# A two-layer token mixer on one core: weight decode without TensorE, and chunk 1's inverse in 16x16 blocks

## Chip, core and metric

The kernel runs on one core of a Trainium2 chip. The metric is the device time of one execution in microseconds. An execution's span runs from its first to its last instruction in the profile. The engines are TensorE (PE; PEld its weight loads), VectorE (DVE), ScalarE (ACT), GpSimd (POOL) and SyncE (SP), which issues most of the DMAs.

## What is computed

Three stages follow one another for 4 x 768 = 3072 tokens with 8 heads of 48 values, 384 in all:

```python
for t in range(S):                                   # S = 768, per batch and head
    y[t] = q[t] @ state                              # k_n = k / (|k| + 1e-6)
    v_old = state.T @ k_n[t]
    state = state + beta[t] * outer(k_n[t], v[t] - v_old)
h = y @ w_in                                         # 384 x 2048
g = where(h >= 1, h, where(h <= -1, 0, (h + 1)**2 / 4))
x = g @ w_out                                        # 2048 x 384
xn = x / sqrt(mean(x*x) + 1e-6) * rms_g
out = (silu(xn @ w_gate) * (xn @ w_val)) @ w_out2    # 1536 wide
```

The weights are float64. The kernel gets them as 64-bit integers and rebuilds from each a float32 and its split into two parts for TensorE: hi, the value rounded to the matmul's format, and lo, the rest.

## The kernel before

**Chunks.** The 768 steps are done in 12 chunks of 64. Per chunk, each of two batch pairs (a unit u = 2 * chunk + pair) goes through the same steps: a_ss and a_coef (norms of k, factors), ka_load and a_gram (Gram matrix of k on TensorE, scaled by nn into al and written to memory as scr_a), an inverse of the unit triangular matrix, a_mz and a_mw (blocks of the inverse, two small TensorE steps), b_load, b_q, b_vn, b_gs (products with state and queries, masked by VectorE), b_tr (the inverse applied), b_x (the chunk's output), b_ds (the new state) and b_xT (transpose to the layer's layout: hi part xh by ScalarE, rest xl by VectorE). Chunk after chunk depends on the state.

**Inverses.** inverse(g) (L510) takes 32x32 blocks of two or four units: 31 steps of two operations on GpSimd over (31 - j)(j + 1) elements. inv0 (L455) is for chunk 0 alone: 16x16 blocks, 15 steps of two operations on VectorE, and the step from 16 to 64 rows is done in b_tr by small matmuls with off, y and z (L644 to L670). Chunk 1 is inverse(1), with a_mz and a_mw behind it.

**First layer.** m1(j, f) works on the tokens of chunk j and 128 of the 2048 columns: nine matmuls into hps (three each of hi*hi, hi*lo, lo*hi), ScalarE's two passes and VectorE's maximum w_ for the activation, a rounding g and its rest, then nine matmuls into acc. The 16 tiles f of a chunk run in order, and chunk j + 1 only behind chunk j. hps has two buffers, given back by w_.

**Weight decode.** w_dec(1, f, i) makes the first layer's 32 weight pieces (128 x 384), w_dec(2, f, i) the second layer's 36, which go back to memory (w2d) and are read again later. Per piece: ScalarE writes the scaled high word y and, into every second 16-bit value of a, its half-precision form with sign and exponent (L275, L276). VectorE shifts y left by 3 and ors in a (L286), masks out the exponent (L287) and multiplies the low word by it (L297, for the second layer L290 and L291 on a copy of the piece that a second load shifts by 16 bits, L271). For the first layer ScalarE then rounds y to hi (L300), TensorE forms y - hi + lo in PSUM by three matmuls with identities (L315 to L317, wlo) and ScalarE or VectorE copies that to lo (L320, L322).

**Order.** Nothing is scheduled at run time: the class Flow plays the stages in Python when the program is built, with a cost and an engine per stage, priorities, and counted buffers, and writes each engine's instructions in the order that comes out. An engine runs its instructions in that order, so one that waits holds up all that stand behind it. In idle time before the first layer TensorE gets dummy matmuls (warm, L866). A stage can name a second engine (alt), and Flow takes the one that is free first.

After the last chunk the second layer runs over six blocks of 512 tokens (m2_l1, m2_l2), with its weights read back from memory.

Of the kernel before, what the change touches and what calls it, by code (L numbers as in the profile page):

```python
# [23 lines left out]
C = 64  # L24
# [30 lines left out]
class Flow:  # L55
# [30 lines left out]
    def start(self, p):  # L86
        key, st, i = p[1], p[3], p[4]
        t = self.free.get(st.eng, 0.0)
# [11 lines left out]
        return t  # L100
# [60 lines left out]
def kernel_body(  # L161
# [14 lines left out]
    stg = ctx.enter_context(tc.tile_pool(name="stg", bufs=4))  # L176
# [54 lines left out]
    def consts2():  # L231
# [19 lines left out]
    def w_dec(n, f, i):  # L251
        if n == 2:
            needs = [("w_dec", 1, NF1 - 1, 1)]
        else:
            needs = [("a_gram", EARLY - 1)] if f + SK * i > 14 else []
        if n == 1:
            needs = needs + ([("inv0", 1 if f + SK * i < 9 else 19)] if f + SK * i >= 4 else [])
        me = ("w_dec", n, f, i)
        mem = "wp" if n == 1 and f + SK * i < 10 else "stg"
        yield S("SP", (1, 1.09) if n == 1 else (2, 2.18), needs, (mem,) * n)  # L260
# [814 lines left out]
```

## Time and profile before

| | us |
|---|---|
| median of 3 runs | 1155.97 (1154.07 to 1157.64) |
| span of the profiled execution | 1152.4 |
| PE busy in the span | 1107.5 (96%) |
| DVE / ACT / POOL busy | 661.8 / 569.9 / 286.3 |

The page gives the profiled execution's span and no total of its own; the runs lie 1.7 to 5.2 us above it. Busy is the time in which an engine executes something; in stretches of the span the shares differ a great deal, so the rows below are by stretch. A row of the timeline has start, length, engine, line, operation, output <- input, shapes and, in brackets, idle time before it with what ended it.

### The profile page before, as it was taken

What the parts mean: (1) busy time and instruction counts of PE and PEld (TensorE: products, weight loads), DVE (VectorE), ACT (ScalarE), POOL (GpSimd) and SP (SyncE); (2) the same over time, 40 slices, a digit from 0 to 9 for tenths busy, and PEclk for the clock granted to TensorE, in tenths of its full rate; (3) what the DMA queues carried; (4) which work ended last, traced back from release to release, by engine and by line L of the source; (5) the groups of instructions that cost most, each with busy time, mean ns of one, the idle gap of its engine ahead of it and who ended that gap; (6) DMA issues with size and microseconds to landing.
All of it is one profiled execution on the core that took longest, in us unless ns stands there. A gap on an engine that the chain in (4) does not pass through costs nothing.

```text
span 1152.4 us, 27191 instructions
## 1 busy us (share of the span) xinstructions
PE 1107.5 (96%) x11224; PEld 996.4 (86%) x11224; DVE 661.8 (57%) x1337; ACT 569.9 (49%) x1360; POOL 286.3 (25%) x479
## 2 busy tenths in 40 slices
PE   8979999999999999999999999999999999999998
PEld 7857888899998999899999999788888888888887
DVE  6797876786877876785775453443433333333333
ACT  4677877765765767567665464222212122122212
POOL 3282865858348114811000000000000000000000
PEclk9989999999999999999999999999999999999999
DMA  7945587784786556385440564001001010010000
GB/s 219 285 143 138 148 262 197 231 208 153 185 224 185 128 199 181 114 206 172 151 148 2 183 207 167 10 23 37 19 1 46 10 37 19 1 46 10 28 1 28
DMA packets 165099, 136.97 MB, mean 119 GB/s; under 512 B 115056, under 2 KB 126064, under 8 KB 164976
## 3 DMA queue, kind: packets, MB, share of 16 engines
q1 hardware_dynamic: 141536, 132.31, 38.2%
q10 hardware_dynamic: 23440, 2.93, 1.7%
q8 instruction: 88, 1.44, 0.5%
q14 instruction: 35, 0.29, 0.1%
HBM read 100.88 MB, written 34.34 MB: 117 GB/s over the span
## 4 chain that ended last, share of the span: by engine, by line
PE 74%; DVE 11%; ACT 4%; POOL 3%; DMA 3%; issue 2%; SPq 1%; DVEq 0%; POOLq 0%; ACTq 0%
PE acc L736 9%; PE gv L736 8%; PE gv L737 8%; PE gv L738 8%; PE acc L737 8%; PE acc L738 8%; PE hps L736 4%; PE hps L737 4%; PE hps L738 4%; PE gs L623 2%; POOL xi L536 2%; PE px L691 2%; POOL tmp L530 2%; PE tr L678 1%; DVE da L287 1%
## 5 line engine op out<-in xcount | busy, mean ns | idle before, releaser
L752 ACT ACTIVATE xh<-fix 128x512 fp32r<-128x512 f32 x72 | 45.5, 632 | 333.7 <-PE acc L738 328.4
L753 DVE TENSOR_TENSOR xl<-fix,xh 128x512 fp32r<-128x512 f32 x72 | 49.9, 694 | 270.6 <-ACT xh L752 270.6
L736 PE MATMUL hps<-xh,w 128*128 128x256 f32 x576 | 167.5, 291 | 9.9 <-DVE w__1065 L773 2.2
L737 PE MATMUL acc<-g,w 128*128 128x256 f32 x576 | 164.7, 286 | 10.6 <-DVE g L781 10.4
L736 PE MATMUL acc<-g,w 128*128 128x256 f32 x576 | 167.8, 291 | 2.7 <-ACT g L779 2.7
L736 PE MATMUL gv<-fix,w 128*128 128x512 f32 x432 | 168.2, 389 | 0.7 <-DVE fix L978 0.7
L737 PE MATMUL gv<-fix,w 128*128 128x512 f32 x432 | 168.1, 389 | 0.0
L738 PE MATMUL gv<-fix,w 128*128 128x512 f32 x432 | 168.1, 389 | 0.0
L737 PE MATMUL hps<-xl,w 128*128 128x256 f32 x576 | 164.2, 285 | 0.0
L738 PE MATMUL hps<-xh,w 128*128 128x256 f32 x576 | 163.9, 285 | 0.0
L738 PE MATMUL acc<-g,w 128*128 128x256 f32 x576 | 163.5, 284 | 0.0
L769 ACT ACTIVATE s<-hps 128x256 f32<-128x256 f32 x192 | 73.6, 384 | 108.3 <-PE hps L738 104.2
L736 PEld LDWEIGHTS hps<-xh,w 128*128 128x128 f32 x576 | 111.2, 193 | 13.7 <-DVE w__1065 L773 2.6
L737 PEld LDWEIGHTS acc<-g,w 128*128 128x128 f32 x576 | 110.7, 192 | 13.0 <-DVE g L781 12.9
L530 POOL TENSOR_TENSOR tmp<-nt,xi 128x87 f32<-128x87 f32 (+21 forms) x186 | 104.4, 561 | 54.5 <-DMA nt<-scr_a 40.4
L736 PEld LDWEIGHTS acc<-g,w 128*128 128x128 f32 x576 | 110.4, 192 | 6.1 <-ACT g L779 2.9
L536 POOL TENSOR_TENSOR xi<-xi,tmp 128x87 f32<-128x87 f32 (+21 forms) x186 | 110.4, 594 | 14.6
L737 PEld LDWEIGHTS hps<-xl,w 128*128 128x128 f32 x576 | 111.4, 193 | 0.3 <-DVE xl L732 0.3
L738 PEld LDWEIGHTS hps<-xh,w 128*128 128x128 f32 x576 | 111.3, 193 | 0.0
L738 PEld LDWEIGHTS acc<-g,w 128*128 128x128 f32 x576 | 110.7, 192 | 0.0
L770 ACT ACTIVATE s<-s,vhalf 128x256 f32<-128x256 f32 x192 | 97.9, 510 | 6.2
L736 PEld LDWEIGHTS gv<-fix,w 128*128 128x128 f32 x432 | 81.1, 188 | 17.8 <-DVE fix L978 1.1
(747 smaller groups left out, 2156.5 us busy)
## 6 DMA issues: line engine op xcount, KB each, us to landing
wst<-in_w SPq DMA_DIRECT2D x68, 384.0 KB, 4.6
w2d<-wst SPq DMA_DIRECT2D x36, 384.0 KB, 4.1
w<-w2d SPq DMA_DIRECT2D x36, 384.0 KB, 6.0
wsv<-in_w SPq DMA_DIRECT2D x36, 383.5 KB, 5.5
kvb<-in_kv SPq DMA_DIRECT2D x22, 384.0 KB, 5.5
kt<-in_kqT SPq DMA_DIRECT2D x24, 256.0 KB, 4.2
scr_a<-al SPq DMA_DIRECT2D x24, 256.0 KB, 3.9
qs<-in_kqT SPq DMA_DIRECT2D x48, 128.0 KB, 4.3
```

The costliest lines, as they stand in the source:

```text
L287: nc.vector.tensor_scalar(out=a, in0=yf, scalar1=0xFF800000, scalar2=None, op0=ALU.bitwise_and)
L530: nc.gpsimd.tensor_tensor(out=tv, in0=nt[:, m:32, j:m].to_broadcast([w, n, m]), in1=x[:, j:m, 0:m].to_broadcast([w, n, m]), op=ALU.mult,)
L536: nc.gpsimd.tensor_tensor(out=x[:, m:32, 0:m], in0=x[:, m:32, 0:m], in1=tv, op=ALU.add)
L623: nc.tensor.matmul(out=ps[half(b), h, 0:n], lhsT=kt[u][half(1 - b), 4 * k + h, :], rhs=qs[p][half(1 - b), b, 4 * k + h, 0:n], start=True, ...
L691: nc.tensor.matmul(out=ps[half(b), h, 0:D], lhsT=t[:, 0:C], rhs=v, start=True, stop=True)
L736: nc.tensor.matmul(out=out, lhsT=wh, rhs=xh, start=first, stop=False, skip_group_check=shared)
L737: nc.tensor.matmul(out=out, lhsT=wh, rhs=xl, start=False, stop=False, skip_group_check=shared)
L738: nc.tensor.matmul(out=out, lhsT=wl, rhs=xh, start=False, stop=last, skip_group_check=shared)
L752: nc.scalar.activation(out=hi, in_=src, func=ACTF.Copy)
L753: nc.vector.tensor_tensor(out=lo, in0=src, in1=hi.bitcast(F32), op=ALU.subtract)
L769: nc.scalar.activation(out=s, in_=ps, func=IDENTITY_SAT240, scale=240.0)
L770: nc.scalar.activation(out=s, in_=s, func=ACTF.Square, bias=vhalf, scale=1.0 / 480.0)
```

## The change

- Decode: ScalarE writes both halves of a: the upper as before, and into the lower 16 bits a third pass that scales the low word to three bits (L266 of the new text). One shift-or then gives the whole float32. hi is rounded by ScalarE or VectorE (alt), and VectorE subtracts: lo = y - hi. The mask, the multiplication, the three matmuls, the copy from PSUM, the second load and the zeroing of a are gone; both layers use the same code. The staging pool has 3 buffers, not 4.
- Chunk 1: inv0 becomes inv16(c) for c = 0 and 1. For chunk 1 its 15 steps run on GpSimd; b_tr takes the 16-row path for both chunks; inverse(1), a_mz and a_mw of chunk 1 are gone.
- a_gram's scaling al for later chunks may run on VectorE in one operation instead of ScalarE's eight.
- Flow: priorities of w_dec and a small change of how start times are counted. The order of all engines comes out anew.

```diff
@@ class Flow
-    CHAIN = {"b_tr": 4, "b_x": 4, "b_xT": 4, "inverse": 2, "a_mz": 4, "a_mw": 4}
+    CHAIN = {"b_tr": 4, "b_x": 4, "b_xT": 4, "inverse": 3, "inv16": 2, "a_mz": 4, "a_mw": 4}
...
-        t = self.free.get(st.eng, 0.0)
+        t = 0.0
...
-        return t
+        return max(t, self.free.get(st.eng, 0.0))
@@ w_dec
-        yield S("SP", (1, 1.09) if n == 1 else (2, 2.18), needs, (mem,) * n)
+        yield S("SP", (1, 1.09), needs, (mem,))
...
-            sv = stg.tile([128, 4 * DM], U16, name="wsv", tag="wst")
-            nc.sync.dma_start(out=sv[:, 0:4 * DM - 2], in_=w2[f, :, DM * i:DM * i + DM].bitcast(U16)[:, 1:4 * DM - 1])
...
-        nc.scalar.activation(out=y.bitcast(F32), in_=wf[:, :, 1], func=ACTF.Copy, scale=2.0**-112)
-        nc.scalar.activation(out=a.bitcast(F16).rearrange("p (n t) -> p n t", t=2)[:, :, 1], in_=wf[:, :, 1], func=ACTF.Copy, scale=2.0**-60)
+        ends = a.rearrange("p (n o) -> p n o", o=1).bitcast(U16)
+        nc.scalar.activation(out=y.bitcast(F32), in_=w_hi, func=ACTF.Copy, scale=2.0**-112)
+        nc.scalar.activation(out=ends[:, :, 1].bitcast(F16), in_=w_hi, func=ACTF.Copy, scale=2.0**-60)
+        nc.scalar.activation(out=ends[:, :, 0], in_=w_lo, func=ACTF.Copy, scale=0.874 * 2.0**-29, bias=0.5)
...
-        nc.vector.scalar_tensor_tensor(out=yf, in0=y, scalar=3, in1=a, op0=ALU.logical_shift_left, op1=ALU.bitwise_or)
-        nc.vector.tensor_scalar(out=a, in0=yf, scalar1=0xFF800000, scalar2=None, op0=ALU.bitwise_and)
...
-        nc.vector.scalar_tensor_tensor(out=lo, in0=w0, scalar=2.0**-52, in1=a.bitcast(F32), op0=ALU.mult, op1=ALU.mult)
+        nc.vector.scalar_tensor_tensor(out=y, in0=y, scalar=3, in1=a, op0=ALU.logical_shift_left, op1=ALU.bitwise_or)
         dac.append(a)
-        yield S("ACT", 0.41)
-        nc.scalar.activation(out=hi, in_=y.bitcast(F32), func=ACTF.Copy)
+        yield S("ACT", 0.41, alt=[("DVE", 0.35)])
+        if fl.eng == "ACT":
+            nc.scalar.activation(out=hi, in_=y.bitcast(F32), func=ACTF.Copy)
+        else:
+            nc.vector.tensor_copy(hi, y.bitcast(F32))
+        yield S("DVE", 0.5, (), (), ("dec",))
+        nc.vector.tensor_tensor(out=lo, in0=y.bitcast(F32), in1=hi.bitcast(F32), op=ALU.subtract)
...
-        nc.tensor.matmul(out=ps, lhsT=ident, rhs=y.bitcast(F32), start=True, stop=False)
-        nc.tensor.matmul(out=ps, lhsT=ineg_r, rhs=hi, start=False, stop=False)
-        nc.tensor.matmul(out=ps, lhsT=ident_r, rhs=lo, start=False, stop=True)
@@ a_gram
-            yield S("ACT", 1.65, [("a_coef", g)], ("wp" if ew else "al",), ("at",))
+            yield S("ACT", 1.65, [("a_coef", g)], ("wp" if ew else "al",), ("at",), alt=[("DVE", 0.6)])
@@ inv16 (was inv0)
+    def inv16(c):
+        us = (2 * c, 2 * c + 1)
+        name, eng = ("POOL", nc.gpsimd) if c else ("DVE", nc.vector)
...
-            eng = nc.scalar if k in (1, 3, 5) else nc.sync
-            eng.dma_start(out=nt[o:o + 16], in_=scr_a[0][o:o + 16, :, :, c:c + 16].rearrange("t u h s -> (u h) t s"))
+            q = nc.scalar if k in (1, 3, 5) else nc.sync
+            q.dma_start(out=nt[o:o + 16], in_=scr_a[c][o:o + 16, :, :, r:r + 16].rearrange("t u h s -> (u h) t s"))
...
-            yield S("DVE", 0.37 + n * m * 2 / 960)
+            yield S(name, 0.36 + n * m * 0.004 if c else 0.37 + n * m * 2 / 960)
@@ b_tr
-        if c == 0:
+        if c < 2:
...
+            for b in range(2):
+                nc.scalar.activation(out=qs[p][half(b), b, :, C:C + D], in_=ps[0][half(b), :, 0:D], func=ACTF.Copy)
@@ the list of work
-        fl.add(PG[0] + 6, inv0)
+        fl.add(PG[0] + 6, inv16, 0)
...
-                fl.add(p0 + 6, inverse, g)
+                fl.add(p0 + 6, *((inverse, g) if g > 1 else (inv16, 1)))
...
-            if a:
+            if a > 1:
                 att(p0, a, ((-8, a_mz), (-5, a_mw)))
...
-                fl.add(f + SK * i + (-14), w_dec, 1, f, i)
+                fl.add(f + SK * i - 5, w_dec, 1, f, i)
```

TensorE's order at the entry of the first layer, before; xps is the transpose of a unit, ds its new state, hps the first tile:

```order
L691 MATMUL px<-z,qs 64x48 x16
L705 MATMUL ds<-z,kvb 48x48 x16
L723 MATMUL xps<-ident,xs 128x128 x3
L705 MATMUL ds<-z,kvb 48x48 x16
L315 MATMUL wlo<-dy,ident 128x384
L316 MATMUL wlo<-w,ineg_r 128x384
L317 MATMUL wlo<-w,ident_r 128x384
```

and with the change, up to the first tile:

```order
L702 MATMUL xps<-ident,xs 128x128 x3
L636 MATMUL tr<-z,y 32x48 x16
L684 MATMUL ds<-z,kvb 48x48 x16
L670 MATMUL px<-z,qs 64x48 x16
L684 MATMUL ds<-z,kvb 48x48 x16
L702 MATMUL xps<-ident,xs 128x128 x3
L401 MATMUL gk<-ka 64x64 x48
L715 MATMUL hps<-xh,w 128x256
```

The weight groups between the transposes and the tiles (another one follows before the first hps, and more between the tiles) are gone, and Gram matrices stand there. Further on, the first a_mw of chunk 2 stood ahead of the ninth tile of the first layer's chunk 1 and stands ahead of the fifth.

VectorE's order around xl, the rest of a unit's transpose, before; L286, L287 and L297 are one piece's decode:

```order
L732 TENSOR_TENSOR xl<-xps,xh 128x3x128
L286 SCALAR_TENSOR_TENSOR dy<-dy,da_100 128x384
L287 TENSOR_SCALAR da_100<-dy 128x384
L297 SCALAR_TENSOR_TENSOR w<-wst,da_100 128x384
L712 TENSOR_TENSOR qs<-ds,qs 48x8x48 x2
L732 TENSOR_TENSOR xl<-xps,xh 128x3x128
L712 TENSOR_TENSOR qs<-ds,qs 48x8x48 x2
```

and with the change; nt_715 is the copy of chunk 1's inverse that GpSimd makes in x_625:

```order
L274 SCALAR_TENSOR_TENSOR dy<-dy,da_100 128x384
L280 CAST w<-dy 128x384
L282 TENSOR_TENSOR w<-dy,w 128x384
L457 COPY nt_715<-x_625 128x256
L711 TENSOR_TENSOR xl<-xps,xh 128x3x128
L691 TENSOR_TENSOR qs<-ds,qs 48x8x48 x2
L412 TENSOR_TENSOR al<-gk,nn 128x512 x3
```

Between the two units' xl the copy of chunk 1's inverse has come in, and the scalings al of later chunks stand behind.

ScalarE's order where chunk 0's inverse is applied (z), with the change; the DMA row is three of the loads of chunk 1's blocks:

```order
L264 ACTIVATE dy<-wst 128x384
L265 ACTIVATE da_98<-wst 128x384
L266 ACTIVATE da_98<-wst 128x384
L627 ACTIVATE z<-tr 128x384
L352 ACTIVATE kk<-kk 128x384 x4
L443 DMA nt_715<-scr_a_556 16x16x16 x3
L641 ACTIVATE z<-tr 128x384
```

Before, chunk 1's blocks were loaded by SyncE alone, and nothing but a rounding stood between these two z.

## Rows read from the trace of the kernel before

**Rows 1.** Stretches: length, busy us (instructions) of PE, PEld, DVE, ACT, POOL; PEclk, DMA share, GB/s

```profile
0.00:58.50 58.50, 50.73 (x842) 45.33 (x843) 42.17 (x114) 32.77 (x71) 19.42 (x50) 1.00 0.84 254
58.50:159.00 100.50, 87.01 (x1075) 74.76 (x1074) 78.85 (x151) 78.20 (x211) 69.59 (x110) 0.95 0.58 163
159.00:703.00 544.00, 524.76 (x7339) 508.28 (x7338) 379.86 (x827) 356.37 (x896) 197.30 (x321) 0.99 0.61 177
703.00:1152.40 449.40, 445.02 (x1976) 368.09 (x1974) 160.92 (x247) 102.52 (x183) 0.00 (x0) 1.00 0.06 21
```

**Rows 2.** TensorE's timeline: first tiles of chunks 0 and 1, two weight groups

```profile
58.53 0.28 PE L736 MATMUL hps<-xh,w 128*128 128x256 f32 x1
...
88.59 0.81 PE L315 MATMUL wlo<-dy,ident 128*128 128x384 f32 x2
...
89.59 0.81 PE L315 MATMUL wlo<-dy,ident 128*128 128x384 f32 x2
...
158.97 0.28 PE L736 MATMUL hps<-xh,w 128*128 128x256 f32 x1
```

**Rows 3.** Line L317 in 58.5 to 159: count, duration min/median/max, starts

```profile
L317 PE MATMUL wlo<-w,ident_r x24: 331/335/522, 58.4 to 140.3; 128*128 128x384 f32 x24
```

**Rows 4.** VectorE's waits in 58.5 to 159: us, times, longest

```profile
DVE g L781 <- ACT g L779: 5.9, 4, 3.2
DVE w L322 <- PE wlo L317: 5.8, 5, 4.3
```

**Rows 5.** SyncE's timeline: loads of chunk 1's blocks

```profile
43.27 2.64 SPq L521 DMA_DIRECT2D nt<-scr_a  x4
```

**Rows 6.** GpSimd's timeline: chunk 1's inverse starts; the next starts and ends

```profile
48.75 0.25 POOL L530 TENSOR_TENSOR tmp<-nt,xi 64x31 f32<-64x31 f32 x1 [27.37 <-DMA nt<-scr_a]
49.08 0.26 POOL L536 TENSOR_TENSOR xi<-xi,tmp 64x31 f32<-64x31 f32 x1
...
118.90 0.25 POOL L530 TENSOR_TENSOR tmp<-nt,xi 128x31 f32<-128x31 f32 x1 [2.71 <-DMA nt<-scr_a]
...
160.59 0.25 POOL L536 TENSOR_TENSOR xi<-xi,tmp 128x31 f32<-128x31 f32 x1
```

**Rows 7.** VectorE by line in 58.5 to 159: busy us, mean ns | idle before

```profile
L297 DVE SCALAR_TENSOR_TENSOR w<-wst,da 128x384 fp32r<-128x384 uint32 x20 | 14.9, 746 | 0.7
L286 DVE SCALAR_TENSOR_TENSOR dy<-dy,da 128x384 uint32<-128x384 uint32 x20 | 14.8, 739 | 0.4 <-ACT da L276 0.4
L287 DVE TENSOR_SCALAR da<-dy 128x384 uint32<-128x384 uint32 x20 | 11.0, 551 | 0.7
L322 DVE CAST w<-wlo 128x384 fp32r<-128x384 f32 x10 | 5.5, 551 | 5.9 <-PE wlo L317 5.8
...
L633 DVE TENSOR_TENSOR qs<-gs,mask 64x256 f32<-64x256 f32 x8 | 3.3, 419 | 0.1
...
L732 DVE TENSOR_TENSOR xl<-xps,xh 128x384 fp32r<-128x384 f32 x3 | 1.5, 541 | 0.0
```

**Rows 8.** ScalarE by line in 58.5 to 159

```profile
L276 ACT ACTIVATE da<-wst 128x384 f16<-128x384 f32 x22 | 13.9, 633 | 0.0
L445 ACT ACTIVATE al<-gk,nn 128x64 f32<-128x64 f32 x64 | 13.7, 367 | 2.6 <-DVE nn L404 2.6
L275 ACT ACTIVATE dy<-wst 128x384 f32<-128x384 f32 x22 | 12.1, 550 | 2.2 <-PE wlo L315 2.2
L300 ACT ACTIVATE w<-dy 128x384 fp32r<-128x384 f32 x20 | 10.3, 523 | 4.1 <-DVE dy L286 4.0
```

**Rows 9.** Line L447, the al that VectorE makes: min/median/max ns

```profile
L447 DVE TENSOR_TENSOR al<-gk,nn x4: 681/691/692, 10.4 to 37.6; 128x512 f32<-128x512 f32 x4
```

**Rows 10.** VectorE's timeline: a shift-or during GpSimd's inverse, and one without

```profile
77.55 0.97 DVE L286 SCALAR_TENSOR_TENSOR dy<-dy,da 128x384 uint32<-128x384 uint32 x1
...
95.14 0.55 DVE L286 SCALAR_TENSOR_TENSOR dy<-dy,da 128x384 uint32<-128x384 uint32 x1
```

**Rows 11.** TensorE's timeline: the first a_mw of chunk 2

```profile
183.98 1.20 PE L569 MATMUL mg<-tx,g 32*32 32x32 f32 x64
```

More of the change, by code (lines that the diff above doesn't have):

```diff
@@ L252, in w_dec @@
         if n == 2:
-            needs = [("w_dec", 1, NF1 - 1, 1)]
+            needs = [("m1", 0, NF1 - 1)]
         else:
@@ L256, in w_dec @@
         if n == 1:
[L257 to L260 removed]
+            needs = needs + ([("inv16", 0, 1 if f + SK * i < 9 else 19)] if f + SK * i >= 4 else [])
+        mem = "wp" if n == 1 and f + SK * i < 13 else "stg"
+        yield S("SP", (1, 1.09), needs, (mem,))
         if mem == "wp":
@@ L309, in w_dec @@
-        yield S("PE", 1.0, (), (bank,), ("dec",))
-        if pre:
-            fl.pre += 1
-            ps = accp.tile([128, 512], F32, name="wlo", tag=f"acc{fl.pre % 2}")[:, 0:DM]
-        else:
-            ps = ap_.tile([128, DM], F32, name="wlo", tag="at")
-        nc.tensor.matmul(out=ps, lhsT=ident, rhs=y.bitcast(F32), start=True, stop=False)
-        nc.tensor.matmul(out=ps, lhsT=ineg_r, rhs=hi, start=False, stop=False)
-        nc.tensor.matmul(out=ps, lhsT=ident_r, rhs=lo, start=False, stop=True)
@@ L318, in w_dec @@
-        yield S("ACT", 0.45, (), (), (bank,), alt=[("DVE", 0.58)])
-        if fl.eng == "ACT":
-            nc.scalar.activation(out=lo, in_=ps, func=ACTF.Copy)
-        else:
-            nc.vector.tensor_copy(lo, ps)
-        w1t[f, i] = t
+        yield S("SP", (1, 1.09), (), (), ("stg",), lag=3.0)
+        w2d[f, i] = dram.tile([128, 2, DM], F32, name=f"w2d{f}_{i}", tag=f"w2d{f}_{i}")
+        nc.sync.dma_start(out=w2d[f, i], in_=t.bitcast(F32))
     def w_in(f, i, pool_):
@@ L652, in b_tr @@
                     nc.tensor.matmul(out=py[half(b), h, :], lhsT=o[half(b), h, :], rhs=dt[half(b), h, :], start=True, stop=True)
-            if u == 0:
-                inv["y"] = p1.tile([128, 2, H, C], F32, name="y", tag="ka")
+            if p == 0:
+                inv["y"] = p1.tile([128, 2, H, C], F32, name="y", tag="y")
             yield S("ACT", 0.38, [("b_tr", u, 0)], ("wt",))
@@ L668, in b_tr @@
                         )
-                yield S("ACT", 0.38, (), (), ("at",) + (("ka",) if u else ()) if k == 2 else ())
-                nc.scalar.activation(out=z, in_=ps[0][:, :, 0:D], func=ACTF.Copy)
-            us0[u] = z
+                if k < 2:
+                    yield S("ACT", 0.38)
+                    nc.scalar.activation(out=z, in_=ps[0][:, :, 0:D], func=ACTF.Copy)
+            end = ("at",) + (("y",) if p else ())
+            if c == 0:
+                yield S("ACT", 0.38, (), (), end)
+                nc.scalar.activation(out=z, in_=ps[0][:, :, 0:D], func=ACTF.Copy)
+                us0[u] = z
+                return
+            yield S("ACT", 0.76, (), (), end + ("wt",))
+            for b in range(2):
+                nc.scalar.activation(out=qs[p][half(b), b, :, C:C + D], in_=ps[0][half(b), :, 0:D], func=ACTF.Copy)
             return
-        yield S("PE", 1.27, [k for v in (u, u ^ 1) for k in (("a_mw", v), ("b_gs", v, 0, i), ("b_gs", v, 1, i), ("b_vn", v))], ("at",), ("wt",))
+        yield S("PE", 1.27, [k for v in (u, u ^ 1) for k in (("a_mw", v), ("b_gs", v, 0, 1), ("b_gs", v, 1, 1), ("b_vn", v))], ("at",), ("wt",))
         ps = ap_.tile([128, H, C], F32, name="tr", tag="at")
@@ L787, in m1 @@
         else:
[L788 to L789 removed]
+            yield S("PE", 1.08, [("w_dec", 1, f, 1)], ("acc",), ("g", "wp") if j == NB - 1 else ("g",), dp=SK)
         m1_l2(j, f)
```

142 lines of the change are left out of this document (57 added, 85 removed).

## Prediction

> **What bounds the kernel now.** I read the stretches first, then the waits of the engines inside the worst stretch, then single rows. The stretches [rows 1] cut the 1152.4 us at three rows of TensorE [rows 2]: the first matmul of the first layer's chunk 0 (58.53), the first of its chunk 1 (158.97), and the second layer's first at 703, where the third stretch ends. The reader is to see that the stretches are bound by different things. The last one has TensorE busy for 445.02 of 449.40 us. In the third, 524.76 of 544.00 us are busy, so at most 19.2 us could be won there without less work. The second stretch is the odd one: 100.50 us for one chunk of the first layer, of which the third stretch does eleven in 544.00. TensorE is busy 87.01 us in it, but weight groups are part of that: 24 have their last matmul in it, one of them at the very border [rows 3], so I count 23, and one group is 1.00 us from its first matmul to that of the next [rows 2]. VectorE is busy 78.85 us, ScalarE 78.20, GpSimd 69.59: nothing is saturated, and the four engines wait for each other in turn. VectorE's waits [rows 4] name the partners: 5.8 us for the three matmuls of a weight group, 5.9 us for ScalarE's rounding of g. The change takes hold in this stretch, so the sum is made by stretches.
>
> **The change, part by part.**
>
> *The way to the first matmul (58.5 us).* Removed are nine weight groups on TensorE, but they stood in time that dummy matmuls fill anyway: nothing. VectorE's decode before the inverse of chunk 0 is shorter by the mask, which the chain behind feels as 2 to 3 us. Against it stand two new in-order waits that the order shows. On ScalarE the three loads of chunk 1's blocks stand ahead of chunk 0's z. They wait until the scaled Gram blocks have landed in memory; the loads that now do the same on SyncE are issued at 43.27 [rows 5] and feed GpSimd at 48.75 [rows 6]. On VectorE the copy of chunk 1's inverse stands ahead of the second xl, without which the first matmul's partner cannot run. GpSimd does that inverse now in 30 operations of at most 64 elements; its first two, of 31 elements, take 0.25 us and start 0.33 us apart [rows 6], and I allow 0.37 on the mean: some 11 us, so it ends near 59.5. Copy and xl (0.54 [rows 7]) bring the first layer to about 60: **+1.5 us**, bounds -2 (the copy never waits) and +4 (the loads land 3 us later).
>
> *Chunk 0 of the first layer (100.5 us).* TensorE loses 23 groups of 1.00 us and gains about 4 us of small matmuls (chunk 1's 16-row steps less its 32-row ones), so its own work falls from 87.0 to 68. ScalarE loses the eight-fold al (13.7), most of the roundings (15 of 20, at 0.523: 7.8) [rows 8] and its copies from wlo. The third pass costs at most the 0.633 us of the second, which has the same input and also writes 16-bit values two apart; between that and the first pass's 0.550 I take 0.633. For the 14 groups that the new order leaves behind the first tile, three passes are 14 x 1.816 = 25.4 us against 26.0 now. ScalarE falls below 57 us. It stops being a partner to wait for.
>
> VectorE is what remains. Busy time removed in the stretch: the three decode operations of 20 groups and ten copies from PSUM, 14.8 + 11.0 + 14.9 + 5.5 = 46.2; the four products behind a_mw, priced as a mask (0.419), 1.7 [rows 7]; second-layer decode that now comes later, one group and a half, about 3. Together 50.9. Added, by counting VectorE's new order from the second xl to the sixteenth w_: 18 groups with shift-or (0.739) and subtraction (two inputs in SBUF like L297, so 0.746), 15 roundings (as L287, 0.551): 35.0; eight al at 0.691 [rows 9]: 5.5; chunk 2's eight masks and four subtractions, which came later, at 0.419: 5.0; chunk 1's dt, y and m, priced as al: 2.9. Together 48.4. So 78.85 - 50.9 + 48.4 = 76. **VectorE's work in this stretch hardly changes; what changes is that it no longer stops for TensorE.** GpSimd corrects this a little. A shift-or takes 0.97 us while GpSimd runs an inverse and 0.55 while it does not [rows 10]; xl, which reads PSUM, has a mean of 0.541 [rows 7]. Chunk 1's inverse now runs before the stretch; the 32-row one for chunks 2 and 3 moves into it from 118.9 to 160.6 [rows 6]. I expect it from about 75 to 117, over 11 of the 18 groups, not nearly all of them: 74 us. Bounds: 64 (none meets GpSimd) and 79 (all do).
>
> Idle time of VectorE is now 100.5 - 78.85 = 21.65 us. The 5.8 us for weight groups goes, and most of the waits for ScalarE should too; I keep 4 us for the last tiles, where TensorE's 2.2 us a tile is the pace. Bounds 2 and 21.65. The stretch becomes 74 + 4 = 78: **-22.5 us**, bounds 66 and 100.
>
> The Trainium skill (SBUF — State Buffer, "Who interferes with whom") says that a VectorE operation with two SBUF inputs, or in a two-port mode, and a GpSimd operation that reads SBUF exclude each other for the whole instruction. This trace agrees on which operations suffer, but shows a mean loss of some 0.19 us in an operation, not a whole GpSimd instruction. The rule speaks against this change, since the new subtraction and rounding are of the exposed kinds and the PSUM copy that they replace was not. With the row's loss the stretch is 78 us; with a full block of 0.6 us for each of 33 operations it would be some 90.
>
> *Chunks 1 to 11 (544 us).* TensorE has the same tiles and the same attention steps here. ScalarE trades 96 al pieces for 35 third passes, VectorE takes 12 al and loses one of four decode operations, and one load of 384 KB in two goes. All of it lies beside TensorE. I take **-3 us** of the 19.2 us that it idles; bounds -10 and +7.
>
> *Second layer (449.4 us).* Untouched: 0.
>
> Sum: 60 + 78 + 541 + 449.4 = 1128.4 us of span, 24 us less. The page records no total beside its span; the median of the runs, 1155.97, lies 3.6 us above the span, which I take as start and end. So **1132 us**.
>
> **Rivals.**
>
> *TensorE sets the stretch after all.* If VectorE's idle time and most of the meeting with GpSimd vanish, the stretch falls to TensorE's 68 us and the later ones gain 6: 60 + 68 + 538 + 449.4 + 3.6 = **1119**. For it: ScalarE is relieved by a quarter and more, and chunk 1 is there 30 us sooner. Against it: the 76 us of VectorE's work.
>
> *Nothing gained.* VectorE's work is the same, and its 21.65 us of waiting may only change partners: the rounding and subtraction wait for ScalarE's three passes, y and dt for TensorE. 60 + 95.7 + 544 + 449.4 + 3.6 = **1153**.
>
> *Full blocking by GpSimd*, the rule above: 60 + 90 + 543 + 449.4 + 3.6 = **1146**. The Trainium skill's page on SBUF, named above, is where this comes from. For it: 0.97 against 0.55 us in the worst rows. Against it: the group means.
>
> *Slower: chunk 2 comes too late.* TensorE's first a_mw of chunk 2 now stands ahead of the fifth tile of chunk 1, before of the ninth. It needs the 32-row inverse. In the trace it runs at 183.98 [rows 11], 65.1 us after that inverse's first operation. I expect the fifth tile at 60 + 78 + 13 = 151, so the inverse has to start by 86; I put its start near 75. Every microsecond later stops TensorE in order, and the gain of 24 is gone at 110. With a start at 118.9 as now, the a_mw runs at 184, 33 us late: **1165**. For it: SyncE's queue holds four loads behind chunk 1's round trip through memory. Against it: that trip starts at 60, not 90.
>
> *The change not doing what it says* can be seen in the order: 58 of the 68 roundings went to VectorE, and 119 dummy matmuls stand where 80 did, so no shorter way to the first tile is to be had. The weight matmuls are really gone.
>
> **How the numbers follow.** Forecast (1123 to 1142) 0.50, TensorE's pace 0.22, full blocking 0.12, nothing gained 0.09, chunk 2 late 0.07. A change within 0.3% (3.5 us: 1152.5 to 1159.4) can't be told from none here. Faster: the first three, 0.84, and a third of the fourth, 0.03: 0.87. Same: the rest of the fourth and a little of the last, 0.07. Slower: 0.06. The low end takes the stretch at 66, the lead-in unchanged and -6 later: 58.5 + 66 + 538 + 449.4 + 3.6 = 1115.5, and 4 us more for the later bound of -10: 1111. The high end is just short of no change, 1151; beyond it lie nothing gained and late chunk 2, below it little.
>
> **What would show each step.** Right: no matmul into wlo; first layer's first tile at 58 to 62; its chunk 1 from 132 to 144; VectorE busy over 85% in between with waits of a few us; shift-or still 0.7 to 0.8 us where GpSimd runs; later stretches within 7 us. Wrong: the first tile after 65 (the in-order waits cost more), chunk 1 before 130 (TensorE's pace) or after 150 (waits only changed partners), an a_mw of chunk 2 that TensorE waits for, or third passes above 0.7 us.

## The result and the profile after

The changed kernel takes **1121.62 us** (median of 4 runs, 1119.69 to 1123.47) against 1156.62 for the kernel before beside it: ratio **0.971**, 95% interval 0.969 to 0.974, 35 us less. The profiled execution has a span of 1120.4 us (1152.4 before) and took 1122.15.

The same four stretches as in [rows 1], in the same columns, cut at the changed kernel's own rows (first tile of chunk 0, first tile of chunk 1, second layer):

```profile
0.00:66.07 66.07, 56.42 (x1012) 53.61 (x1012) 49.16 (x129) 40.03 (x85) 21.35 (x60) 0.95 0.84 261
66.07:140.59 74.52, 64.65 (x1049) 61.01 (x1046) 70.44 (x146) 53.65 (x119) 45.15 (x67) 0.93 0.68 182
140.59:670.94 530.35, 519.32 (x7276) 505.90 (x7275) 369.83 (x783) 353.66 (x837) 195.72 (x312) 0.99 0.54 155
670.94:1120.40 449.46, 444.89 (x1975) 368.09 (x1973) 161.03 (x247) 102.41 (x183) 0.00 (x0) 1.00 0.06 21
```

The way to the first tile is 7.5 us longer (58.5 to 66.07), chunk 0's stretch 26.0 shorter (100.5 to 74.52), chunks 1 to 11 13.65 shorter (544.0 to 530.35), the second layer the same. The sum is the 32 us. In chunk 0's stretch VectorE is now busy for 70.44 of 74.52 us (95%); before, no engine came near that, TensorE with 87.01 of 100.50 us was the busiest. The rows that answer to [rows 7] and [rows 8], VectorE and ScalarE by line in 66.07 to 140.59 (busy us, mean ns | idle before):

```profile
L282 DVE TENSOR_TENSOR w<-dy,w 128x384 fp32r<-128x384 f32 x18 | 13.1, 733 | 0.4
L274 DVE SCALAR_TENSOR_TENSOR dy<-dy,da 128x384 uint32<-128x384 uint32 x18 | 11.9, 670 | 1.0 <-ACT da L266 1.0
L280 DVE CAST w<-dy 128x384 fp32r<-128x384 f32 x15 | 8.3, 550 | 0.2
...
L412 DVE TENSOR_TENSOR al<-gk,nn 128x512 f32<-128x512 f32 x8 | 5.3, 676 | 0.0
```

```profile
L265 ACT ACTIVATE da<-wst 128x384 f16<-128x384 f32 x14 | 8.8, 629 | 0.0
L266 ACT ACTIVATE da<-wst 128x384 uint16<-128x384 uint32 x14 | 8.7, 619 | 0.0
...
L264 ACT ACTIVATE dy<-wst 128x384 f32<-128x384 f32 x14 | 7.6, 541 | 0.5 <-DVE w L282 0.4
```

VectorE's 5.8 us of waits for weight groups [rows 4] are gone with the groups, and the decode's own idle time is under 2 us. The shift-or L274, the rounding L280 and the subtraction L282 stand where three operations and a copy stood.

The time lost ahead of the first tile ends in one chain through three engines. GpSimd's timeline (start us, us), with the first and the last of the 30 operations of chunk 1's inverse, and the next operation on GpSimd:

```profile
50.64 0.22 POOL L449 TENSOR_TENSOR tmp<-nt,x 128x15 f32<-128x15 f32 x1 [22.50 <-DMA wst<-in_w]
...
63.23 0.22 POOL L455 TENSOR_TENSOR x<-x,tmp 128x15 f32<-128x15 f32 x1
63.41 0.83 POOL L582 TENSOR_TENSOR kvb<-kvb,n__540 128x384 f32<-128x384 f32 x1
```

VectorE's, whose copy L457 waits 5.45 us for that inverse with the second xl (L711) behind it, and TensorE's, where a Gram tile (gk) waits for xl, with the first tile behind it:

```profile
57.47 0.56 DVE L282 TENSOR_TENSOR w<-dy,w 128x384 fp32r<-128x384 f32 x1
63.48 0.99 DVE L457 COPY nt<-x 128x256 f32<-128x256 f32 x1 [5.45 <-POOL x L455]
64.40 0.54 DVE L711 TENSOR_TENSOR xl<-xps,xh 128x384 fp32r<-128x384 f32 x1
```

```profile
65.00 1.15 PE L401 MATMUL gk<-ka 64*64 64x64 f32 x32 [2.92 <-DVE xl L711]
66.07 0.39 PE L715 MATMUL hps<-xh,w 128*128 128x256 f32 x1
```

A second delay stands beside it. The second unit's transpose itself runs 3.9 us later on TensorE than in the kernel before (the first row is of before, the second of the changed kernel), so without the copy the way would still have been longer:

```profile
55.11 0.55 PE L723 MATMUL xps<-ident,xs 128*128 128x128 f32 x3 [0.29 <-ACT xs L694]
```

```profile
58.98 0.90 PE L702 MATMUL xps<-ident,xs 128*128 128x128 f32 x3
```

### The profile page after: what moved, and what is told of

Same layout as the page of the kernel before. It is cut to its first block, busy times and chain, and to the rows that moved or that the text cites. A ratio compares the mean times of both kernels' runs of the same rounds, so it can differ in the third digit from the quotient of the medians.

```text
span 1120.4 us, 27049 instructions
## 1 busy us (share of the span) xinstructions
PE 1085.3 (97%) x11302; PEld 988.6 (88%) x11302; DVE 650.5 (58%) x1302; ACT 549.8 (49%) x1224; POOL 262.2 (23%) x438
## 4 chain that ended last, share of the span: by engine, by line
PE 79%; DVE 11%; issue 2%; ACT 2%; DMA 2%; SPq 2%; POOL 1%; POOLq 0%; DVEq 0%
PE acc L715 9%; PE acc L716 9%; PE acc L717 9%; PE gv L715 9%; PE gv L717 9%; PE gv L716 9%; PE hps L715 5%; PE hps L716 5%; PE hps L717 5%; PE warm L842 2%; PE gs L593 2%; DVE dy L274 2%; DVE g L760 1%; PE px L670 1%; PE tr L657 1%
## 5 line engine op out<-in xcount | busy, mean ns | idle before, releaser
L748 ACT ACTIVATE s<-hps 128x256 f32<-128x256 f32 x192 | 72.9, 380 | 101.7 <-PE hps L717 94.4
L506 POOL TENSOR_TENSOR xi<-xi,tmp 128x31 f32<-128x31 f32 (+15 forms) x155 | 96.7, 624 | 12.1
L500 POOL TENSOR_TENSOR tmp<-nt,xi 128x31 f32<-128x31 f32 (+15 forms) x155 | 88.7, 572 | 42.5 <-DMA nt<-scr_a 30.8
```

The lines of the kernel that those rows point to most:

```text
L500: nc.gpsimd.tensor_tensor(out=tv, in0=nt[:, m:32, j:m].to_broadcast([w, n, m]), in1=x[:, j:m, 0:m].to_broadcast([w, n, m]), op=ALU.mult,)
L506: nc.gpsimd.tensor_tensor(out=x[:, m:32, 0:m], in0=x[:, m:32, 0:m], in1=tv, op=ALU.add)
L748: nc.scalar.activation(out=s, in_=ps, func=IDENTITY_SAT240, scale=240.0)
```

## Experiments

Open were: what made the first tile late (theory 1: VectorE's in-order wait at the copy); which half of the change gives the 26 us (theory 2: the decode); where the 13.65 us of chunks 1 to 11 come from (theory 3: al on VectorE; theory 6: the order of the steps alone); whether VectorE is the bound in the stretch (theory 4). Theory 5, on GpSimd's order, came up on the way. Each of the twelve kernels was timed against the kernel before on the same chip, whose median there was 1153.99 to 1155.28 us (1156.62 beside the changed kernel); medians of two rows can differ by that much without cause. The stretches are of one execution each. The last columns are of chunks 1 to 11: VectorE busy, and TensorE idle (length less busy).

| kernel | median us | ratio, 95% interval | first tile | chunk 0 | chunks 1-11 | DVE busy | PE idle |
|---|---|---|---|---|---|---|---|
| before | 1155.97 | 1 | 58.5 | 100.5 | 544.1 | 379.9 | 19.2 |
| changed | 1121.62 | 0.971, 0.969-0.974 | 66.1 | 74.5 | 530.3 | 369.8 | 11.0 |
| e1 copy on GpSimd | 1124.08 | 0.974, 0.971-0.976 | 64.4 | 75.0 | 535.4 | 362.0 | 11.8 |
| e2 decode, old inverse | 1147.29 | 0.995, 0.993-0.997 | 63.6 | 78.4 | 554.0 | 378.4 | 23.3 |
| e3 inverse, old decode | 1152.63 | 0.998, 0.996-0.999 | 74.5 | 92.2 | 536.7 | 366.5 | 15.0 |
| e4 al on ScalarE | 1134.01 | 0.982, 0.978-0.985 | 67.2 | 77.8 | 534.7 | 359.4 | 17.2 |
| e5 subtraction twice | 1137.77 | 0.985, 0.983-0.987 | 69.2 | 85.1 | 531.3 | 369.2 | 12.5 |
| e6 third pass twice | 1128.33 | 0.978, 0.975-0.980 | 65.8 | 76.3 | 531.0 | 368.8 | 11.5 |
| e7 rounding on ScalarE | 1126.88 | 0.976, 0.974-0.978 | 63.7 | 75.7 | 536.2 | 357.9 | 13.0 |
| e9 tile before Gram tile | 1130.08 | 0.979, 0.977-0.982 | 63.8 | 72.5 | 545.4 | 367.7 | 17.4 |
| e11 before, al on VectorE | 1169.02 | 1.013, 1.010-1.015 | 59.2 | 99.6 | 556.4 | 384.6 | 25.9 |
| c2 = e9 + kvb early | 1124.54 | 0.974, 0.971-0.977 | 62.9 | 72.8 | 535.9 | 370.2 | 14.1 |
| c3 = c2 + roundings | 1128.60 | 0.977, 0.974-0.979 | 59.6 | 75.0 | 542.0 | 372.5 | 17.9 |
| e12 2nd subtraction twice | 1139.28 | 0.988, 0.984-0.992 | 64.7 | 72.9 | 549.8 | 391.8 | 26.7 |

Only e5, e6 and e12 keep the changed kernel's order of instructions; every other edit makes the planner (Flow) write a new one. Up to chunk 1 e12 issues what the changed kernel issues, and shows 64.7 and 72.9 where that has 66.1 and 74.5: differences of under 2 us in a stretch of one execution are not read as effects.

### e1: the copy of chunk 1's inverse on GpSimd

```diff
-        yield S("DVE", 0.35)
-        nc.vector.tensor_copy(nt, x.rearrange("p t s -> p s t"))
+        yield S(name, 0.35)
+        eng.tensor_copy(nt, x.rearrange("p t s -> p s t"))
```

> The changed kernel with one edit: the copy that turns chunk 1's finished inverse round stands on GpSimd, behind the additions that it waits for, and no longer on VectorE. Theory 1 (VectorE stands still in its own order: 5.5 us at this copy, and the second xl and then TensorE's gk of chunk 2 behind it): the first layer's first tile moves from 66.1 to between 61 and 63 us, and the whole by about as much, to 1117 to 1119 us. Rival (the way to the first tile is longer by loads, by ScalarE's order and by TensorE's own waits, and VectorE's wait only stands beside them): first tile at 65 to 67, time within 1 us of 1121.6.

Half right. VectorE no longer stands still, and the second xl moves from 64.40 to 60.69. The first tile comes only at 64.43 (61 to 63 was expected): in TensorE's order the third Gram tile of the next inverse stands before it, and within that tile TensorE stops for 1.82 us. "issue" says that the profile shows nothing that it waited for; the cause stays open.

```profile
60.69 0.56 DVE L711 TENSOR_TENSOR xl<-xps,xh 128x384 fp32r<-128x384 f32 x1 [0.57 <-ACT xh L709]
```

```profile
63.47 1.03 PE L401 MATMUL gk<-ka 64*64 64x64 f32 x27 [1.82 <-issue]
64.43 0.39 PE L715 MATMUL hps<-xh,w 128*128 128x256 f32 x1
```

The 1.6 us of the first tile, less than one execution can tell, are not in the total either. In the profiled execution (1126.05; two of the other three are at 1121.8 and 1122.1, like the changed kernel) chunks 1 to 11 are 5.1 us longer, 4.3 of them as busy time of TensorE (523.6 against 519.3). The stretches from chunk 1 on show the place (length, busy PE, PEld, DVE, ACT, POOL, then PEclk): at 266.1 the granted clock falls to 0.50, the lower of its two levels (1.2 of 2.4 GHz), for 17.1 us.

```profile
139.40:266.10 126.70, 120.01 (x1731) 115.75 (x1729) 97.95 (x200) 94.75 (x221) 85.27 (x142) 1.00 0.65 182
266.10:283.20 17.10, 16.41 (x276) 15.20 (x276) 10.76 (x24) 6.44 (x15) 4.54 (x6) 0.50 0.48 108
283.20:674.80 391.60, 387.14 (x5306) 379.09 (x5303) 253.26 (x553) 255.22 (x606) 104.36 (x164) 1.00 0.49 146
```

Right before it TensorE had stood idle for 2.42 us, as VectorE waited for GpSimd's kvb, which came at 263.93 in this order:

```profile
266.06 0.53 PE L815 MATMUL rps<-sr,ones_r 128*128 128x256 f32 x1 [2.42 <-DVE qs L603]
```

### e2: the new decode with chunk 1's old inverse

The kernel before with the changed w_dec, its place in the order and the choice of engine for al; inverse(1), a_mz and a_mw of chunk 1 as before.

> The kernel before with the new decode (both layers, its new place in the order) and the choice of VectorE for al, but with chunk 1 still by the 32-row inverse and the two small products. Theory 1 (chunk 1's 16-row inverse costs the 7.5 us ahead of the first tile): first tile back at 58 to 60. For the stretch of chunk 0, two theories: the decode alone gives the gain (VectorE no longer stops for TensorE): stretch 74 to 80 us, total 1110 to 1122; or chunk 1's earlier inverse is needed as well, since chunk 1's xps, which came at 128.8 before, would again come some 25 us later than in the changed kernel: stretch 85 to 100, total 1125 to 1145.

The decode alone brings the stretch to 78.4 us, nearly all of it (theory 2). Yet the total gains 7.5 us only. Chunk 1's 16 tiles were done quickly (the last starts at 187.09), chunk 2's attention was not ready, and its steps then ran with few tiles to fill the gaps: 30.6 us in which TensorE is busy for 24.71.

```profile
142.00:187.10 45.10, 40.65 (x435) 39.07 (x434) 38.74 (x85) 32.64 (x78) 25.09 (x41) 1.00 0.60 177
187.10:217.70 30.60, 24.71 (x623) 22.41 (x621) 21.83 (x36) 17.33 (x45) 22.81 (x38) 0.88 0.91 256
```

Chunk 2's first a_mw is at 191.68 here, at 150.57 in the changed kernel, and its first tile at 217.7, which is 217.2 in the kernel before. This is the prediction's "chunk 2 comes too late", and it is what the decode does without the other half of the change. The first tile at 63.6 (58 to 60 was expected) says that chunk 1's inverse is not the only thing that makes it late: here the second transpose runs at 54.04, earlier than before, but four Gram tiles stand between it and the first tile, and TensorE is at them from 56.93 to 63.6.

### e3: the new inverse with the first layer's old decode

The changed kernel with the first layer's w_dec as before (three matmuls into wlo); one weight buffer fewer.

> The changed kernel with the first layer's decode as before (mask, product, three matmuls into wlo, its old place in the order; one weight buffer of 34 fewer, to make room), the second layer's decode as changed. Theory 2 (the gain in chunk 0's stretch is the decode's: no stop of VectorE for weight groups, 23 us of matmuls less): the stretch is 92 to 102 us, the total 1138 to 1156. Rival (chunk 1's inverse in 16x16 blocks gives most of it, since it takes GpSimd's long 32-row steps out of the start and brings chunk 1's attention sooner): stretch 76 to 86, total 1122 to 1132. The chunks 1 to 11 tell a third thing: 528 to 534 us if the first layer's decode, which is over by then, has nothing to do with their gain of 13.6.

Theory 2 holds: 92.2 us in the stretch, total 1152.63, though the first tile is at 74.5, later than in any other (four Gram tiles and four weight groups stand between the second transpose, at 65.65, and it). Apart the two halves gain 7.5 (e2) and 2.1 us (e3, both against 1154.75 beside them); together 35. (The second layer's new decode and the choice of engine for al are in both.) Chunks 1 to 11 take 536.7, above the 528 to 534 expected.

### e4 and e11: al on ScalarE, and al on VectorE in the kernel before

```diff
-            yield S("ACT", 1.65, [("a_coef", g)], ("wp" if ew else "al",), ("at",), alt=[("DVE", 0.6)])
+            yield S("ACT", 1.65, [("a_coef", g)], ("wp" if ew else "al",), ("at",))
```

> The changed kernel with one edit: al, the scaled Gram tiles, of chunk 4 on always by ScalarE in eight pieces of 0.37 us, as before, never by VectorE in one of 0.68. Theory 3 (the 13.6 us that chunks 1 to 11 gained came from ScalarE, which no longer holds g and s back for 2.9 us at each al): these chunks go back to 538 to 544 us, total 1129 to 1135. Rival (the gain there comes from the lighter second-layer decode and from chunk 2 and 3 being ahead): these chunks stay at 527 to 534, total 1118 to 1125. The way to the first tile stays at 65 to 67 by both.

534.7 lies between the two theories: 4.4 us, not 13.65. The total, 1134.0, lies in theory 3's range, but of its 12.4 us the profiled execution (1130.93) shows 8.8, and only these 4.4 in chunks 1 to 11. e11 makes the opposite edit in the kernel before.

> The kernel before with one edit: al of chunk 4 on may be done by VectorE in one operation of 0.68 us where that is the earlier, as in the changed kernel, in place of eight ScalarE pieces of 0.35. Theory 3 (of the 13.6 us that chunks 1 to 11 gained, about 4 to 6 are al's): chunks 1 to 11 fall from 544 to 537 to 541; chunk 0's stretch, where ScalarE loses 13.7 us, to 92 to 99; total 1140 to 1150. Rival (al is worth nothing by itself; the orders that the planner finds differ by some 15 us in these chunks, whatever edit makes it plan anew, as the runs so far show with 530 to 545): chunks 1 to 11 anywhere from 532 to 550, with no tie to al.

Theory 3 falls as a price of al by itself. With al on VectorE chunks 1 to 11 take 556.4 us, 12.3 more than before and beyond the rival's 550 too, and the kernel is 1.3% slower. In the table VectorE is busy for 4.7 us more there, and TensorE idle for 6.7 more; the other 5.7 us are busy time of TensorE. What of this is al's and what the new order's isn't shown.

### e5, e6 and e7: is VectorE the bound in chunk 0's stretch?

```diff
+        for _ in range(2 if n == 1 else 1):
             nc.vector.tensor_tensor(out=lo, ..., op=ALU.subtract)
```

> The changed kernel with the first layer's subtraction on VectorE issued twice, into the same tile, the order of all else untouched (the planner is not told). 18 more operations of 0.73 us stand in chunk 0's stretch: 13.1 us. Theory 4 (VectorE, 95% busy there, is the bound): the stretch grows from 74.5 by 11 to 14, to 86 to 89 us, and the first tile moves by some 1 to 5 us as well. Rival (TensorE, 64.6 us busy there, or ScalarE sets it just as much): the stretch grows by less than 7.

The stretch grows by 10.6 us, just under the 11 to 14 expected, and VectorE's busy time in it by 9.7 (the row is e5's stretch of chunk 0, in the columns of the first fence). TensorE's busy time grows too, by 8.4 us, at a granted clock of 0.82 against 0.93. But VectorE's idle time went only from 4.1 to 4.9 us: it is as full as before, and the slower TensorE stands beside its work.

```profile
69.20:154.30 85.10, 73.03 (x1049) 69.22 (x1046) 80.17 (x161) 54.71 (x122) 44.71 (x66) 0.82 0.58 159
```

> The changed kernel with the first layer's third ScalarE pass (16-bit ends from the low words) issued twice, the order untouched. 14 more passes of 0.62 us stand in chunk 0's stretch: 8.7 us on ScalarE, which is 53.7 of 74.5 us busy there. Theory 4 (VectorE is the bound, ScalarE has slack): the stretch grows by 0 to 3 us. Rival (VectorE and ScalarE take turns, each waits for the other): it grows by 6 to 9. The total grows by as much and by what the way to the first tile adds (0 to 4).

e6 does to ScalarE's third pass what e5 does to the subtraction. ScalarE's busy time grows by 11 us (64.61), the stretch by 1.8. So in this stretch work added to VectorE is paid in full, work added to ScalarE hardly. The median total rose by 6.7 us, though; the profiled execution, the fastest of the four at 1124.35, shows 2.2 of them, and where the others lose the rest isn't shown. e7 takes work away from VectorE (`yield S("ACT", 0.41)` for the rounding, without the alternative).

> The changed kernel with every rounding of the decode on ScalarE (no choice of VectorE). In chunk 0's stretch VectorE loses 15 of 0.55 us (8.3) and ScalarE gains 15 of 0.52 (7.8): 62 and 61.5 us. Theory 4 (VectorE is the bound): the stretch falls to 66 to 70, TensorE's 64.6 being the next floor, total 1114 to 1118. Rival (each subtraction then waits for a rounding on the other engine, as the kernel before waited between engines): the stretch stays at 73 to 77, total 1120 to 1126.

The rival is right about the stretch, for another reason: the subtraction L282, which it took to wait for the rounding on the other engine, has 0.0 us of idle time before it. VectorE has 12.4 us less to do, and the stretch is 75.7 us:

```profile
63.70:139.40 75.70, 66.88 (x1038) 62.67 (x1036) 58.00 (x122) 59.47 (x135) 42.79 (x68) 0.89 0.71 181
```

The waits of that stretch in e7 (us, times, longest) show the next limit right behind the first. The steps of chunks 1 and 2 stand in VectorE's and TensorE's order and are waited for. The profile names no releaser for the Gram tile gk; it starts at 128.58, right behind the masks that VectorE makes from 127.63 on, and these stood behind the kvb that VectorE waited 5.9 us for:

```profile
DVE kvb L599 <- POOL kvb L582: 5.9, 1, 5.9
PEld gk L401 <- issue: 5.4, 1, 5.4
ACT w L278 <- DVE dy L274: 5.4, 6, 2.7
PE gk L401 <- issue: 5.3, 1, 5.3
```

```profile
127.63 0.85 DVE L603 TENSOR_TENSOR qs<-gs,mask 64x256 f32<-64x256 f32 x2
```

```profile
128.58 1.23 PE L401 MATMUL gk<-ka 64*64 64x64 f32 x18 [5.27 <-issue]
```

The order is a new one here as well, so e7 does not show what less work on VectorE would bring in the changed kernel's own order.

### e9, c2 and c3: an earlier first tile

e9 is e1 with the third Gram tile's need of the first product:

```diff
-        yield S("PE", 1.27, [("ka_load", x) for x in ...], ("at",), ...)
+        yield S("PE", 1.27, [("ka_load", x) for x in ...] + ([("m1", 0, 0, 0)] if u == 6 else []), ("at",), ...)
```

> The kernel with the copy of chunk 1's inverse on GpSimd, and one edit more: the third Gram tile of chunks 2 and 3 (16 small matmuls) may stand in TensorE's order only behind the first layer's first product. In the run with the copy alone the second xl came at 60.69 instead of 64.40, but TensorE, in order, stood 1.82 us ahead of that Gram tile and did it (1.0 us) before the first product at 64.43. Theory 1 in its new form (two in-order waits one behind the other, VectorE's at the copy and TensorE's at the Gram tile): first tile at 61 to 62.5, 4 to 5 us ahead of the changed kernel. Rival (what TensorE wins is lost to a later inverse of chunks 2 and 3, which starts at 83 and may start by 86 at the latest): chunk 2 from 197 or later instead of 195.7, total 1121 or more. If neither that nor a stop of the clock comes between: 1116 to 1118.

First tile 63.8 (61 to 62.5 was expected), chunk 1 at 136.3, 4.3 us ahead of the changed kernel, and the total is 8 us worse: 1.5 us of the gain are left at chunk 2 (194.2 against 195.7), and chunk 3, in which the clock falls again, takes 66 us. c2 adds `"b_vn": 24` to CHAIN, so that kvb goes first.

> The kernel with the copy on GpSimd and the third Gram tile behind the first product, with one edit more: the scaling of v on GpSimd (kvb) goes ahead of an inverse's steps as soon as its load is there. In that kernel and in the one with the copy alone, chunk 3's kvb stood behind an inverse (263.9 and 268.4), TensorE stopped 2.4 and 2.9 us, and the granted clock was at half for 17.1 and 13.7 us right behind; together their chunks 1 to 11 took 535.4 and 545.4 in place of 530.3. Theory 5 (GpSimd's order made that stop): no stop of over 1 us there, chunks 1 to 11 at 527 to 534; with the first tile at 63 to 65 and the stretch at 72 to 75 the total is 1112 to 1120. Rival (each new order has a stop somewhere): chunks 1 to 11 at 535 to 546, total 1121 to 1133.

The stop in chunk 3 is gone (53.4 us for it), others are there: 535.9, as the rival had it. Total 1124.5, not told from the changed kernel's by the intervals. c3 also moves the first layer's roundings to ScalarE.

> The kernel of the run before this one, with the first layer's roundings all on ScalarE (the second layer's may still be done by VectorE). With the roundings alone on ScalarE the stretch stayed at 75.7 although VectorE had 12 us less to do, since VectorE then waited 5.9 us for GpSimd's kvb and TensorE 5.3 us for a bank that VectorE held. Theory 5 (with GpSimd's order mended the freed time counts): stretch 66 to 71, total 1108 to 1116. Rival (chunk 1's chain of attention steps through all four engines sets the stretch, whichever engine is relieved): stretch 72 to 76, total 1114 to 1125.

Here the first tile is at 59.6, as predicted for the change, so the way there can be had back; chunk 1 begins at 134.6, 6 us earlier than in the changed kernel. Chunk 3 begins at 251.7 against 251.9. The stretch stays at 75.0 with VectorE busy for 57.43: the rival again, with a total above its 1125. None of the twelve is faster than the changed kernel.

### e12: second-layer subtraction twice

```diff
+        for _ in range(n):
             nc.vector.tensor_tensor(out=lo, ..., op=ALU.subtract)
```

> The changed kernel with the second layer's subtraction on VectorE issued twice, the order of all else untouched: 36 operations of some 0.7 us, 25 us of VectorE in chunks 1 to 11, where it is 369.8 of 530.3 us busy (379.9 of 544.1 before). Theory 6 (the lighter second-layer decode has no share in the 13.6 us; what differs is how the planner's order happens to place the attention steps): these chunks take 529 to 534 us, total 1120 to 1126. Rival (that decode's work delays w_ and g, for which TensorE waits): 536 to 545 us, total 1128 to 1136.

Theory 6 falls, and the rival was too mild: 549.8 us. With the order untouched, 22.0 us more of VectorE's work make TensorE idle for 15.7 us more (and busy for 3.8 more). The stretch of chunks 1 to 11, and TensorE's waits in it: w_ and g stand behind decode operations in VectorE's order.

```profile
137.60:687.40 549.80, 523.15 (x7275) 507.63 (x7274) 391.79 (x819) 354.61 (x837) 197.94 (x312) 0.99 0.52 149
```

```profile
PE hps L716 <- DVE w__4189 L753: 5.7, 1, 5.7
PE acc L717 <- DVE g L761: 3.9, 7, 1.9
PE mg L540 <- ACT xs L674: 3.5, 1, 3.5
PE hps L716 <- DVE w__5964 L753: 1.8, 1, 1.8
```

## Why the prediction was right, and where its steps were not

1132 us was forecast, 1111 to 1151 the range; 1121.6 came, just below the forecast's own 1123 to 1142. Three terms of the span were off, by +6, -3.5 and -10.7 us, so part of the agreement is errors that cancel. A fourth was the 3.6 us for start and end: it set a median against the span of the fastest run (1154.07, 1.7 us above its span); behind the change it is 1.75 us for the profiled execution and 1.2 for the median.

**The way to the first tile: +7.5, not +1.5, and beyond the bound of +4.** The two in-order waits were named, and the one on VectorE is the one that bit. ScalarE's was harmless: its loads were issued by 45.30, and z behind them started at 45.40, when TensorE's product for it had ended at 45.18. The step that failed is "it ends near 59.5. Copy and xl (0.54) bring the first layer to about 60". GpSimd's inverse started at 50.64, not 48.75, and took 12.8 us for 30 operations, not 11; it ended at 63.45, 3.95 late. The copy took 0.99 us, for which the sum had nothing, and a Gram tile of 1.07 stood between xl and the first tile, which the prediction had not read from TensorE's order. Together that is the 6 us. The experiments show that this chain is not all. e1 takes the copy out of it (64.4), e9 and c2 the Gram tile too (63.8 and 62.9), and only c3 comes to 59.6. The sum took chunk 0's own steps to be no later than before, but the second unit's transpose is 3.9 us later, at 58.98; in e1, e9 and c2 it is at 58.9 to 60.7, in c3 at 57.1.

**Chunk 0's stretch: -26.0, forecast -22.5, bounds 66 and 100.** The argument held: VectorE's work hardly changes and its stops for TensorE go. The counts were exact (18, 18, 15 and 8 operations, 14 groups on ScalarE), the third pass took 0.619 us in place of 0.633, idle time was 4.1 in place of 4; the work came to 70.4 in place of 74. Of these 3.6 us the shift-or, at 0.670 us and not 0.739, makes 1.2; the rest is not taken apart. What the prediction did not see is that a second limit lies right beside VectorE. It took TensorE's pace to be the only thing behind; with VectorE at 58.0 (e7) and 57.4 (c3) the stretch stays at 75 to 76, though TensorE is busy for 65 to 67 us of it. Both have new orders, so what the next limit is in the changed kernel's own order is not shown.

**Chunks 1 to 11: -13.65, forecast -3, bounds -10 and +7.** The failed step is "All of it lies beside TensorE". It does not: by e12 a microsecond added to VectorE's work costs TensorE 0.7 us of idle time (15.7 for 22.0). The change took 10 us from VectorE there. By the rows of its lines the second layer's decode fell by 11.4 (80.3 to 68.9) and al took 7.5 back; 6.4 more are masks, subtractions and norms of chunks that stand ahead of the border now. If the rate held downwards as well, which no run tests with the order kept, that is an estimated 7 us. TensorE's idle time fell by 8.2. The other 5.4 are busy time: 64 small Gram matmuls now stand ahead of the border, 3.3 us by their rows' sums (14.0 to 10.7); the rest stays open. Across the runs, TensorE idles for 11 to 18 us with VectorE at 358 to 373 and for 19 to 27 at 378 and more (e2's 23.3 holds its stop in chunk 1). That the planner's order by itself moves these chunks is shown as well: e1 and e9, whose edits lie ahead of them, take 5 and 15 us longer than the changed kernel with less of VectorE's work; e4 and e7, which also put work on ScalarE, 4 and 6. How much of the 13.65 is luck of the order isn't settled.

**Second layer: 0, as forecast.** 449.46 against 449.40.

**The rivals.** "Chunk 2 comes too late" had the right mechanism: chunk 2's inverse starts at 83.14, 3 us inside the limit of 86 that the prediction gave, its first a_mw comes 67.4 us later (65.1 was taken), and without the 16x16 blocks it happens (e2). "Nothing gained" is near to what e3 does, for other reasons. In number the measured 1121.6 is nearer to "TensorE sets the stretch after all" (1119) than to the forecast (1132). That is luck: the rival's 68 us for the stretch did not come, and the 6.5 us by which it was missed were made up by chunks 1 to 11, for which it took 6 us and 13.65 came. "Full blocking by GpSimd" is next.

**GpSimd's price was near, the reading of the rule was not.** The prediction said that the trace shows a mean loss and "not a whole GpSimd instruction". It shows just that: in the changed kernel 36 of 38 subtractions (66 to 700 us) that began while a GpSimd operation ran end 0.40 to 0.45 us after its end, whenever they began; 35 of 36 roundings 0.21 to 0.25 us after it. The two other subtractions took their undisturbed 0.54 us and ended first. VectorE's timeline and GpSimd's at the same place:

```profile
96.29 0.76 DVE L280 CAST w<-dy 128x384 fp32r<-128x384 f32 x1
97.09 0.88 DVE L282 TENSOR_TENSOR w<-dy,w 128x384 fp32r<-128x384 f32 x1
```

```profile
96.03 0.81 POOL L500 TENSOR_TENSOR tmp<-nt,xi 128x231 f32<-128x231 f32 x1
96.92 0.64 POOL L506 TENSOR_TENSOR xi<-xi,tmp 128x231 f32<-128x231 f32 x1
```

GpSimd's ends are 96.84 and 97.56, VectorE's 97.05 and 97.97: 0.21 and 0.41 behind. Undisturbed the two take 0.36 and 0.56. So VectorE waits for the rest of one GpSimd operation. The Trainium skill (SBUF — State Buffer, "Who interferes with whom") says that whichever of the two engines issues first has the shared ports for its whole instruction, and that the other blocks fully. The trace agrees. The rival's 0.6 us an operation was too much because only the rest of a short operation is waited for, and not each one meets any: by the means 0.174 us for a subtraction, 0.118 for a shift-or (0.552 undisturbed) and 0.191 for a rounding, 8.1 us for the 51 operations of the stretch.

## What to carry to other kernels

An engine that is 95% busy is a bound against more work, not a promise for less: double one of its operations with the order kept, and also take some away, before you plan on the gain. Work on an engine that "lies beside" the busiest one was not free here, where each takes its instructions in order, so price it by the steps that stand behind it. And when one stage of a pipeline gets faster, work out when the next chunk's inputs are there: here either half of the change alone was worth 2 to 8 us, both together 35.

## What the runs showed of the hardware

A VectorE operation with two inputs in SBUF that starts within a GpSimd operation nearly always waits for its end, a long one's too: the split of g (L760), undisturbed 0.42 us, took 1.50 beside a selection of 1.26 us and ended at 137.77, 0.26 behind it; of 77 such splits (66 to 700 us) 73 end 0.26 to 0.40 us behind. The comparison L752, which reads PSUM, took its usual 0.41 beside GpSimd's L500 at 117.09. VectorE's timeline, then GpSimd's:

```profile
117.09 0.41 DVE L752 TENSOR_TENSOR w__1973<-s,hps 128x256 f32<-128x256 f32 x1
...
136.27 1.50 DVE L760 TENSOR_TENSOR g<-w__2270,g 128x256 fp32r<-128x256 f32 x1
```

```profile
116.83 0.74 POOL L500 TENSOR_TENSOR tmp<-nt,xi 128x207 f32<-128x207 f32 x1
...
136.25 1.26 POOL L486 TENSOR_SCALAR_AFFINE_SELECT xi<-xi 128x1024 f32<-128x1024 f32 x1
```

A stop of 2.42 us of TensorE stood right ahead of 17.1 us at the lower clock (e1), in e9 one of 2.87 ahead of 13.7:

```profile
270.45 1.75 PE L539 MATMUL mg<-tx,g 32*32 32x32 f32 x45 [2.87 <-DVE qs L603]
```

```profile
270.50:284.20 13.70, 13.43 (x267) 12.69 (x269) 9.33 (x21) 7.00 (x16) 4.54 (x6) 0.50 0.47 97
```

TensorE's busy time in chunks 1 to 11 is 523.6 us in e1 and 528.1 in e9, where the changed kernel has 519.3 in nearly the same steps (7276 matmuls against 7308 and 7307; the 31 or so more are one Gram tile, about 1 us). So the slower clock gave away an estimated 3 us in e1, more than the stop itself, and 8 in e9, which is at the lower clock once more from 161.2, for 10.2 us.
